# Attention scores at even steps only, and query scores in four passes a block that DVE adds up

## The chip, the cores and the metric

The kernel runs on one core of one Trainium2 chip. The metric is the device time of one execution in microseconds, median over the runs.

## The reference

Agent attention, then a feed-forward network with gelu on its output. Four batches, 12480 tokens, 128 channels, 49 agents; 2048 hidden units.

```python
def _attn_ref(q, k, v, agents):
    scale = 1.0 / np.sqrt(q.shape[-1])
    def sm(a, b):
        s = scale * (a @ b.transpose(0, 2, 1))
        s = s - s.max(-1, keepdims=True)
        e = np.exp(s)
        return e / (e.sum(-1, keepdims=True) + 1e-09)
    a2k = sm(agents, k)
    agent_v = a2k @ v
    q2a = sm(q, agents)
    return (q2a @ agent_v).astype(np.float32)

def _moe_ref(x, w_in, w_out):
    h = x @ w_in
    g = h * (1.0 / (1.0 + np.exp(-1.702 * h)))
    return (g @ w_out).astype(np.float32)
```

## The kernel before

All engines work in an order that is written out by hand. The unit of work on queries is a group of 960 tokens (13 a batch, 52 in all). For each group the feed-forward network runs over 16 blocks of 128 hidden units, the **steps**; `two_steps(t)` issues two of them, a **double step**, and eight double steps make a **cycle**. The agents' values are multiplied into `w_in` once a batch (`weights_part`), so the up projection takes the softmaxed query scores directly.

In a double step TensorE (PE) does in this order: four matmuls of 480 columns (L407) and four row-tiled ones on 19 rows (L410, the **quad**), the jobs put at the even step, six **downs** (L445: `gh` with `wo_h`, `gl` with `wo_h`, `gh` with `wo_l`, each for two halves of the group) of one of the steps four back, the jobs put at the odd step (`second`), and the six downs of the other step. ACT applies gelu (L420) to the four results and rounds every second one to `gh` (L430); a DMA issued by POOL rounds the others. DVE makes the remainder `gl = g - gh` (L435) of each step, one of the two behind the jobs of the even step and one behind those of the odd step.

The attention work of later groups and of the next batch is put at steps by the table `at`. At step f of a cycle (f = t mod 16):

- query scores for the group after next at `Q_AT` = 12 (first half of its 8 blocks of 120 tokens) and 13 (second half), split into three bf16 parts by four DVE pieces at 8 to 11 (L173, L175); the maximum and its subtraction (`query_shift`, L350 and L352) at 14, exp at the next 0, sums and normalization at 2, transposes (L379) at `P_AT` = 4.
- key scores of the next batch, 13 blocks, each in two halves at the next two free steps, even or odd (`pe_step`); then `key_store`: ACT copies the bank to `score` (L228) and DVE takes the running maximum from the same bank (L225).
- after the last key block its maximum, then values (`key_values`, L284, 8 passes of 258 columns) at steps 6 and 11 of the next six to seven cycles, with `value_pair` (L279, L280) four steps ahead of them into a single buffer `v_pair`; then the weights (L330).

So a batch passes through a key phase (about five cycles, the first in the start), a value phase (about six) and a weights phase (two); the last 13 cycles have no next batch and none of it. Here they are called late cycles.

A score is the sum of six products of bf16 parts, accumulated by six matmuls of 49 columns in one bank; each loads its own weights (the token block):

```python
products = [(x0, 0), (x0, 1), (x0, 2), (x1, 0), (x1, 1), (x2, 0)]
```

The score, key maximum, transposes, values and weights share two PSUM banks (`ps_m`).

Of the kernel before, what the change touches and what calls it, by code (L numbers as in the profile page):

```python
# [8 lines left out]
F32 = mybir.dt.float32  # L9
# [5 lines left out]
ALU = mybir.AluOpType  # L15
AX = mybir.AxisListType

P = 128
TB = 120
KB = 8  # L20
# [7 lines left out]
Q_AT = 12  # L28
E_AT = 0
P_AT = 4  # L30
S_AT = 8
K_AT = 3
V_AT = (6, 11)
V_LAST = 5
R = 30
FIRST_WORDS = 1
FIRST_UP = 2
# [6 lines left out]
def kernel(  # L44
# [10 lines left out]
    nc = tc.nc  # L55
    B, C, N = qT.shape
    A = agT.shape[2]
    F = w_in.shape[1] // 2
    NF = F // P
    NG = N // GT  # L60
    NKG = N // (TB * KB)
# [11 lines left out]
    ps_m = ctx.enter_context(tc.tile_pool(name="ps_m", bufs=2, space=bass.MemoryType.PSUM))  # L73
# [10 lines left out]
    for c in range(2):  # L84
        nc.vector.tensor_add(
            out=sel[:, c * H : c * H + A], in0=ident[:, 0:A], in1=ident[:, H : H + A]
# [3 lines left out]
    for i in range(2):  # L90
        t = const.tile([P, KB, P], F32R, name=f"e_pair{i}")
# [8 lines left out]
    e_sb = const.tile([P, KB, A + 1], F32, name="e_sb")  # L100
# [5 lines left out]
    score = const.tile([P, NKG * KB, A], F32, name="score")  # L106
# [44 lines left out]
    ag_part = const.tile([P, B, 3, A], BF16, name="ag_part")  # L151
# [27 lines left out]
    def scores(b, parts, ps, c):  # L179
        x0, x1, x2 = parts  # L180
        for j in range(c * KB // 2, (c + 1) * KB // 2):
            t = slice(j * TB, j * TB + P)
            o = ps[:, j * A : (j + 1) * A]
            products = [(x0, 0), (x0, 1), (x0, 2), (x1, 0), (x1, 1), (x2, 0)]
            for i, (x, y) in enumerate(products):
                nc.tensor.matmul(  # L186
                    out=o,
                    lhsT=x[:, t],
                    rhs=ag_part[:, b, y, :],
                    start=(i == 0),  # L190
                    stop=(i == len(products) - 1),
                )

    def score_bank():
        ps = ps_m.tile([P, 512], F32, name="ps_m")
        return ps, ps[:TB, : KB * A].rearrange("p (j a) -> p j a", a=A)
# [24 lines left out]
    def running_max(g, s):  # L221
        if g == 0:
            nc.vector.tensor_copy(out=run_max[:TB], in_=s)
        else:
            nc.vector.tensor_tensor(out=run_max[:TB], in0=s, in1=run_max[:TB], op=ALU.max)  # L225

    def key_store(g, s):
        nc.scalar.copy(out=score[:TB, g * KB : (g + 1) * KB, :], in_=s)  # L228
        running_max(g, s)

    def key_max_0(d):
        mx = work.tile([P, A], F32, name="mx", bufs=1)
        nc.vector.tensor_reduce(out=mx[:TB], in_=run_max[:TB].rearrange("p j a -> p a j"), axis=AX.X, op=ALU.max)
        d["mx"] = mx
# [36 lines left out]
    def key_pair(g):  # L271
        sc = score[:TB, g * KB : (g + 1) * KB, :]
        ep = e_pair[g % 2]
        nc.vector.tensor_copy(out=ep[:TB, :, 0:A], in_=sc)
        nc.vector.tensor_sub(out=ep[:TB, :, H : H + A], in0=sc, in1=ep[:TB, :, 0:A].bitcast(F32))
# [67 lines left out]
    def query_load(b, g):  # L343
        t = loads.tile([P, GT + PAD], F32, name="qt", tag="qt", bufs=1)
        nc.sync.dma_start(out=t[:, 0:GT], in_=qT[b, :, g * GT : (g + 1) * GT])
        return t

    def query_shift(s):
        m = work.tile([P, KB], F32, name="m")
        nc.vector.tensor_reduce(out=m[:TB], in_=s, axis=AX.X, op=ALU.max)  # L350
        sd = e_sb[:TB, :, 0:A]
        nc.vector.tensor_tensor(  # L352
            out=sd, in0=s, in1=m[:TB].unsqueeze(2).broadcast_to([TB, KB, A]), op=ALU.subtract
        )
        return sd

# [109 lines left out]
    q_parts = {}  # L466
    scored = {}
    banks = {}
# [5 lines left out]
    def do_key_load(b, g):  # L474
        if b < B and g < NKG:
            kts[b, g] = key_load(b, g)
# [5 lines left out]
    def do_query_load(n):  # L482
        if n < B * NG:
            qts[n] = query_load(*divmod(n, NG))

    def do_key_split(b, g, i):
        if i == 0:
            k_parts[b, g], pieces[b, g] = split(kts.pop((b, g)))
        pieces[b, g](i)
# [7 lines left out]
    def do_key_scores(b, g, c):  # L497
        if c == 0:
            banks[b, g] = score_bank()
        scores(b, k_parts[b, g], banks[b, g][0], c)  # L500

    def do_key_store(b, g):
        key_store(g, banks.pop((b, g))[1])

    def do_key_values(b, g):
        sums[b, g] = key_values(g)
# [5 lines left out]

    def do_query_scores(n, c):
        if n < B * NG:
            if c == 0:
                banks[n] = score_bank()
            scores(n // NG, q_parts[n], banks[n][0], c)

    def do_query_shift(n):
        if n < B * NG:  # L520
            scored[n] = query_shift(banks.pop(n)[1])

    def do_query_exp(n):
        if n < B * NG:
# [57 lines left out]
    for g in range(NKG):  # L582
# [3 lines left out]
        for j in range(KB):  # L586
            nc.tensor.matmul(
                out=acc_ps[:A, : C + 1],
                lhsT=score[:TB, g * KB + j, :],
                rhs=vt[:TB, j, :],  # L590
                start=(g == 0 and j == 0),
                stop=(g == NKG - 1 and j == KB - 1),
# [23 lines left out]
    steps = B * NG * NF  # L616
    per_batch = NG * NF
    at = {}
    pe_steps = {n * NF + f for n in range(B * NG) for f in (Q_AT, Q_AT + 1, P_AT)}

    def put(t, fn):
        at.setdefault(t, []).append(fn)


    def pe_step(t):
        while t in pe_steps:
            t += 1
        pe_steps.add(t)
        return t
# [7 lines left out]
    for b in range(B - 1):  # L637
        s0 = b * per_batch
        done = s0
        for k in range(NKG):  # L640
            t = pe_step(s0 + (11 + 5 * k if b == 0 else K_AT + 11 * k // 2))
            t1 = pe_step(t + 1)
            put(t - 13 if b else max(t - 13, 0), lambda b=b, k=k: do_key_load(b + 1, k))
            begin = max(t - 4, done + 1)
            for i in range(4):
                put(min(begin + i, t - 1 if i < 2 else t1 - 1), lambda b=b, k=k, i=i: do_key_split(b + 1, k, i))
            done = t1
            put(t, lambda b=b, k=k: do_key_scores(b + 1, k, 0))
            put(t1, lambda b=b, k=k: do_key_scores(b + 1, k, 1))
            put(t1 + 1, lambda b=b, k=k: do_key_store(b + 1, k))  # L650
        mx = {}
        put(t1 + 2, lambda mx=mx: key_max_0(mx))
        t = pe_step(t1 + 3)
        put(t, lambda mx=mx: key_max_1(mx))
        t = pe_step(t + 2)
        put(t, lambda mx=mx: key_max_2(mx))
        shift = t + 1

        g0 = (shift + 1 - s0 - E_AT + NF - 1) // NF
        for k in range(NKG):  # L660
            slot = s0 + (g0 + k // 2) * NF + E_AT
            exps.setdefault(slot, []).append(k)
            last = k == NKG - 1
            t = slot + (V_LAST if last else V_AT[k % 2])
            put(min(shift + 3 * k, slot - 1), lambda k=k: key_shift(k, nc.vector.tensor_tensor))
            put(t - 16, lambda b=b, k=k: do_value_load(b + 1, k))
            put(t - 4, lambda b=b, k=k: value_pair(vts.pop((b + 1, k))))
            put(slot + 3 - last, lambda k=k: key_pair(k))
            assert t not in pe_steps
            put(t, lambda b=b, k=k: do_key_values(b + 1, k))  # L670
            put(t + 1, lambda b=b, k=k: do_key_sum(b + 1, k))
        w = {}
        put(t + 2, lambda b=b, w=w: weights_0(accs.pop(b + 1), w))
        t = pe_step(t + 3)
        put(t, lambda w=w: weights_1(w))
        for c in range(F // 512):
            t = pe_step(t + (3 if c else 1))
            assert t < s0 + per_batch + 4 * c - 5, (b, shift - s0, g0, t - s0)
            put(t, lambda b=b, w=w, c=c: weights_part(b + 1, w, c))
    for n in range(B * NG):  # L680
        s0 = n * NF
        if n:
            put(s0 + E_AT, lambda n=n: do_query_exp(n + 1))
            if s0 + E_AT in exps:
                ks = exps[s0 + E_AT]
                put(s0 + E_AT, lambda ks=ks: key_exp(ks[0], len(ks)))
            put(s0 + E_AT + 2, lambda n=n: do_query_sums(n + 1))
            put(s0 + E_AT + 2, lambda n=n: do_query_softmax(n + 1))
        put(s0 + P_AT, lambda n=n: do_query_pairs(n + 1))
        for i in range(4):  # L690
            put(s0 + S_AT + i, lambda n=n, i=i: do_query_split(n + 2, i))
        for c in range(2):
            put(s0 + Q_AT + c, lambda n=n, c=c: do_query_scores(n + 2, c))
        put(s0 + Q_AT + 2, lambda n=n: do_query_load(n + 3))
        put(s0 + Q_AT + 2, lambda n=n: do_query_shift(n + 2))


    E = mybir.EngineType
    g = {}
# [98 lines left out]
```

## Time and profile before

| | |
|---|---|
| median of 3 runs | 2039.23 us (2039.01 to 2040.26) |
| the profiled execution | 2040.92 us |
| its span, first to last instruction | 2039.1 us |
| PE busy, share of the span | 1992.4 us, 98% |
| DVE busy | 1576.9 us, 77% |
| ACT busy | 1440.2 us, 71% |
| POOL busy | 281.4 us, 14% |

Busy time of PE counts a matmul from its start to its modelled end, so it is no measure of how well the array is used; the chain of work that ended last and the starts of instructions in the time line say more. Bf16 passes overlap one another: the pace is read from one start to the next.

### The profile page before, as it was taken

The page shows a single profiled execution, that of the slowest core. Times are in us where ns is not written, and L with a number is a line of the kernel's source. Part 1 is how long each engine was busy: PE and PEld are TensorE (multiplying, and loading weights), DVE is VectorE, ACT ScalarE, POOL GpSimd, SP SyncE. Part 2 cuts the span into 40 slices and gives each one's busy share as a digit, 9 for nine tenths or more (in the row PEclk, how much of TensorE's full clock was granted, in tenths as well). Part 3 has the DMA queues.
Part 4 walks back from the last instruction along what each step waited for, and adds up shares of the span by engine and source line. Part 5 has one row for each costly group of instructions (what it writes and reads, how often), then busy time and mean ns, then how long its engine had stood idle before and what let it go on. Part 6 is the DMA issues. An engine that isn't in the chain of part 4 may idle for free.

```text
span 2039.1 us, 36417 instructions
## 1 busy us (share of the span) xinstructions
PE 1992.4 (98%) x13688; PEld 1525.2 (75%) x13688; DVE 1576.9 (77%) x2025; ACT 1440.2 (71%) x2457; POOL 281.4 (14%) x594
## 2 busy tenths in 40 slices
PE   8789999999999999999999999999999999999999
PEld 7567777777777777777777777777777777777776
DVE  4788888888777879888777888888877776767665
ACT  3256677677776777777776677777777877777775
POOL 3011111111111111111111111111111111111111
PEclk9799999999999999999999999999999999999999
DMA  9645556565455565565555555566545545455443
GB/s 252 180 157 182 180 181 184 172 190 174 159 170 174 181 191 181 173 190 175 170 172 171 180 190 175 170 191 174 170 164 161 178 156 170 155 171 165 161 157 134
DMA packets 129444, 356.00 MB, mean 175 GB/s; under 512 B 15696, under 2 KB 48688, under 8 KB 129268
## 3 DMA queue, kind: packets, MB, share of 16 engines
q0 software_dynamic: 67520, 230.22, 34.4%
q1 hardware_dynamic: 61748, 123.46, 20.9%
q8 instruction: 108, 1.77, 0.4%
q14 instruction: 68, 0.56, 0.1%
HBM read 80.97 MB, written 25.56 MB: 52 GB/s over the span
## 4 chain that ended last, share of the span: by engine, by line
PE 89%; DVE 5%; ACT 2%; DMA 2%; issue 1%; POOL 1%; SPq 0%; ACTq 0%; POOLq 0%; DVEq 0%
PE po L445 53%; PE ph L407 17%; PE ph L410 8%; PE ps_m L186 6%; PE ps_m L284 2%; DVE gl L435 1%; DMA gh<-g 1%; PE ps_m L379 1%; PE ps_m L209 1%; ACT g L420 1%; PE ps_m L330 1%; DVE rest L173 1%; DVE rest L175 1%; POOL score L265 1%; DMA words<-w_in 0%
## 5 line engine op out<-in xcount | busy, mean ns | idle before, releaser
L420 ACT ACTIVATE g<-ph 128x480 f32<-128x480 f32 x1664 | 816.6, 577 | 494.4 <-PE ph L410 489.3
L435 DVE TENSOR_TENSOR gl<-g,gh 128x960 fp32r<-128x960 f32 x832 | 941.3, 1153 | 192.5 <-DMA gh<-g 101.9
L445 PE MATMUL po<-gh,wo_h 128*128 128x480 f32 x1664 | 551.7, 413 | 1.9 <-DMA gh<-g 1.9
L445 PE MATMUL po<-gl,wo_h 128*128 128x480 f32 x1664 | 502.1, 383 | 4.9 <-DVE gl L435 4.3
L445 PE MATMUL po<-gh,wo_l 128*128 128x480 f32 x1664 | 500.2, 382 | 0.0
L426 POOL DMA_DIRECT2D gh<-g x468 | 252.0, 538 | 1689.9 <-ACT g L420 1129.2
L445 PEld LDWEIGHTS po<-gl,wo_h 128*128 128x128 f32 x1664 | 311.6, 189 | 63.0 <-DVE gl L435 14.9
L445 PEld LDWEIGHTS po<-gh,wo_l 128*128 128x128 f32 x1664 | 314.0, 189 | 49.8
L445 PEld LDWEIGHTS po<-gh,wo_h 128*128 128x128 f32 x1664 | 273.2, 189 | 85.4 <-issue 64.8
L407 PE MATMUL ph<-sa,wh 128*128 128x480 f32 x832 | 319.8, 384 | 4.8 <-ACT g L420 3.3
L407 PE MATMUL ph<-sb,wh 128*128 128x480 f32 x832 | 321.6, 386 | 0.0
L430 ACT CAST gh<-g 128x960 fp32r<-128x960 f32 x312 | 311.8, 999 | 9.0
L410 PE MATMUL ph<-rq,wq 19*128 19x480 f32 x1664 | 205.2, 481 | 0.0
L407 PEld LDWEIGHTS ph<-sa,wh 128*128 128x128 f32 x832 | 157.4, 189 | 37.4 <-ACT g L420 11.0
L407 PEld LDWEIGHTS ph<-sb,wh 128*128 128x128 f32 x832 | 157.2, 189 | 35.4 <-ACT g L420 11.6
L410 PEld LDWEIGHTS ph<-rq,wq 19*128 19x128 f32 x1664 | 80.0, 182 | 137.0 <-issue 136.5
L186 PE MATMUL ps_m<-ag_part,rest 128*128 128x49 bf16 x2184 | 130.3, 185 | 6.6 <-DVE rest L175 6.4
L175 DVE TENSOR_TENSOR rest<-rest 128x480 bf16<-128x480 f32 (+1 forms) x182 | 129.8, 719 | 0.4
L186 PEld LDWEIGHTS <-rest 128*128 128x128 bf16 x2184 | 109.4, 97 | 8.4 <-DVE rest L175 7.8
L225 DVE TENSOR_TENSOR run_max<-ps_m,run_max 120x392 f32<-120x392 f32 x36 | 20.4, 567 | 79.3 <-ACT score L228 79.1
L186 PEld LDWEIGHTS <-qt 128*128 128x128 bf16 x1248 | 61.3, 98 | 25.1 <-issue 25.0
L186 PE MATMUL ps_m<-ag_part,qt 128*128 128x49 bf16 x1248 | 74.6, 186 | 0.0
(97 smaller groups left out, 1326.8 us busy)
## 6 DMA issues: line engine op xcount, KB each, us to landing
gh<-g POOLq DMA_DIRECT2D x468, 480.0 KB, 3.6
kt<-kT SPq DMA_DIRECT2D x52, 480.0 KB
qt<-qT SPq DMA_DIRECT2D x52, 480.0 KB
vt<-v SPq DMA_DIRECT2D x52, 480.0 KB
outT<-o SPq DMA_DIRECT2D x104, 240.0 KB
rq<-sa SPq DMA_DIRECT2D x104, 35.6 KB
rq<-sb SPq DMA_DIRECT2D x104, 35.6 KB
sa<-sa SPq DMA_DIRECT2D x104, 28.1 KB
```

Source lines behind the costliest of these rows:

```text
L173: nc.vector.tensor_sub(out=r[:, s], in0=t[:, s], in1=halves(t)[0][:, s])
L175: nc.vector.tensor_sub(out=halves(r)[1][:, s], in0=r[:, s], in1=halves(r)[0][:, s])
L186: nc.tensor.matmul(out=o, lhsT=x[:, t], rhs=ag_part[:, b, y, :], start=(i == 0), stop=(i == len(products) - 1),)
L225: nc.vector.tensor_tensor(out=run_max[:TB], in0=s, in1=run_max[:TB], op=ALU.max)
L284: nc.tensor.matmul(out=ps[:, : 2 * C + 2], lhsT=e_pair[g % 2][:TB, j, :], rhs=v_pair[:TB, j, :], start=(first and j == 0), stop=(last and ...
L407: nc.tensor.matmul(out=ph[k][:, :CH], lhsT=wh[:, cols[i]], rhs=pairs[c], start=True, stop=False)
L410: nc.tensor.matmul(out=ph[k][:, :CH], lhsT=wq[r, cols[i]], rhs=rq[r], start=False, stop=True, tile_position=(k * 32, 0),)
L420: nc.scalar.activation(out=gs[i][:, c, :], in_=ph[k][:, :CH], func=AF.Gelu_apprx_sigmoid)
L426: nc.gpsimd.dma_start(out=gh, in_=g)
L430: nc.scalar.copy(out=gh, in_=g)
L435: nc.vector.tensor_sub(out=gl, in0=g, in1=gh.bitcast(F32))
L445: nc.tensor.matmul(out=po[c][:, :CH], lhsT=lhsT[:, f, :], rhs=rhs[:, c, :], start=(begin and first), stop=(end and last),)
```

## The change

Query scores: a block of 120 tokens gets four passes instead of six, into two columns for each agent (98 columns a block). The high part of the tokens meets agent parts 0 and 1 in one pass of 98 columns, part 2 in one of 49 into the second column; the middle part meets 0 and 1 in one of 98; the low part meets 0 in one of 49. Eight blocks now fill two banks (`score_halves`), and DVE adds the two columns (two `tensor_reduce`) before the maximum. All query scores stand at step 12, the shift at 13, and the next query load at 13.

Key scores: both halves of a block at one even step, from the tables `K_FIRST` and `K_AT`; ACT's copy at the step after, the running maximum one step later still and from `score`. `pe_step` gives even steps alone. Values go to 6 and 10.

```diff
-K_AT = 3
-V_AT = (6, 11)
-V_LAST = 5
+K_FIRST = (10, 16, 22, 26, 32, 38, 42, 48, 54, 58, 62, 66, 70)
+K_AT = (6, 10, 16, 22, 26, 32, 38, 42, 48, 54, 58, 64, 70)
+V_AT = (6, 10)
...
+    def score_halves(b, parts, c):
+        x0, x1, x2 = parts
+        a = ag_part[:, b].rearrange("p i a -> p (i a)")
+        mm = nc.tensor.matmul
+        ps = ps_m.tile([P, 512], F32, name="ps_m")
+        for j in range(KB // 2):
+            t0 = (c * KB // 2 + j) * TB
+            t = slice(t0, t0 + P)
+            o = ps[:, j * 2 * A : (j + 1) * 2 * A]
+            mm(out=o, lhsT=x0[:, t], rhs=a[:, 0 : 2 * A], start=True, stop=False)
+            mm(out=o[:, A:], lhsT=x0[:, t], rhs=a[:, 2 * A :], start=False, stop=False)
+            mm(out=o, lhsT=x1[:, t], rhs=a[:, 0 : 2 * A], start=False, stop=False)
+            mm(out=o[:, 0:A], lhsT=x2[:, t], rhs=a[:, 0:A], start=False, stop=True)
+        return ps[:TB, : KB * A].rearrange("p (j i a) -> p j a i", i=2, a=A)
...
     def key_store(g, s):
         nc.scalar.copy(out=score[:TB, g * KB : (g + 1) * KB, :], in_=s)
-        running_max(g, s)
...
-    def query_shift(s):
+    def query_shift(halves):
+        sd = e_sb[:TB, :, 0:A]
+        for c, s in enumerate(halves):
+            o = sd[:, c * KB // 2 : (c + 1) * KB // 2, :]
+            nc.vector.tensor_reduce(out=o, in_=s, axis=AX.X, op=ALU.add)
         m = work.tile([P, KB], F32, name="m")
-        nc.vector.tensor_reduce(out=m[:TB], in_=s, axis=AX.X, op=ALU.max)
-        sd = e_sb[:TB, :, 0:A]
+        nc.vector.tensor_reduce(out=m[:TB], in_=sd, axis=AX.X, op=ALU.max)
         nc.vector.tensor_tensor(
-            out=sd, in0=s, in1=m[:TB].unsqueeze(2).broadcast_to([TB, KB, A]), op=ALU.subtract
+            out=sd, in0=sd, in1=m[:TB].unsqueeze(2).broadcast_to([TB, KB, A]), op=ALU.subtract
         )
         return sd
...
-    pe_steps = {n * NF + f for n in range(B * NG) for f in (Q_AT, Q_AT + 1, P_AT)}
+    pe_steps = {n * NF + f for n in range(B * NG) for f in (Q_AT, P_AT)}
...
     def pe_step(t):
-        while t in pe_steps:
+        while t % 2 or t in pe_steps:
             t += 1
         pe_steps.add(t)
         return t
...
         for k in range(NKG):
-            t = pe_step(s0 + (11 + 5 * k if b == 0 else K_AT + 11 * k // 2))
-            t1 = pe_step(t + 1)
+            t = s0 + (K_AT if b else K_FIRST)[k]
+            assert pe_step(t) == t
             put(t - 13 if b else max(t - 13, 0), lambda b=b, k=k: do_key_load(b + 1, k))
             begin = max(t - 4, done + 1)
             for i in range(4):
-                put(min(begin + i, t - 1 if i < 2 else t1 - 1), lambda b=b, k=k, i=i: do_key_split(b + 1, k, i))
-            done = t1
-            put(t, lambda b=b, k=k: do_key_scores(b + 1, k, 0))
-            put(t1, lambda b=b, k=k: do_key_scores(b + 1, k, 1))
-            put(t1 + 1, lambda b=b, k=k: do_key_store(b + 1, k))
+                put(min(begin + i, t - 1), lambda b=b, k=k, i=i: do_key_split(b + 1, k, i))
+            done = t
+            for c in range(2):
+                put(t, lambda b=b, k=k, c=c: do_key_scores(b + 1, k, c))
+            put(t + 1, lambda b=b, k=k: do_key_store(b + 1, k))
+            put(t + 2, lambda k=k: running_max(k, score[:TB, k * KB : (k + 1) * KB, :]))
...
         for c in range(2):
-            put(s0 + Q_AT + c, lambda n=n, c=c: do_query_scores(n + 2, c))
-        put(s0 + Q_AT + 2, lambda n=n: do_query_load(n + 3))
-        put(s0 + Q_AT + 2, lambda n=n: do_query_shift(n + 2))
+            put(s0 + Q_AT, lambda n=n, c=c: do_query_scores(n + 2, c))
+        put(s0 + Q_AT + 1, lambda n=n: do_query_load(n + 3))
+        put(s0 + Q_AT + 1, lambda n=n: do_query_shift(n + 2))
```

The order on the engines shows what that moves. On PE, in a key phase before the change, at the border of the two halves of a key block (`rest` and `kt` are parts of the key block, `po0` and `po1` the two output halves):

```order
L186 LDWEIGHTS rest_7213
L186 MATMUL ps_m_7259<-ag_part_106,rest_7213 128x49
L445 MATMUL po0_7153<-gh_7151,wo_h_101 128x480
L445 MATMUL po1_7154<-gh_7151,wo_h_101 128x480
L445 MATMUL po0_7153<-gl_7222,wo_h_101 128x480
L445 MATMUL po1_7154<-gl_7222,wo_h_101 128x480
L445 MATMUL po0_7153<-gh_7151,wo_l_102 128x480
L445 MATMUL po1_7154<-gh_7151,wo_l_102 128x480
L186 LDWEIGHTS kt_6848
L186 MATMUL ps_m_7259<-ag_part_106,kt_6848 128x49
```

After the change, at the end of a key block (L463 is the former L445):

```order
L186 LDWEIGHTS rest_7197
L186 MATMUL ps_m_7322<-ag_part_106,rest_7197 128x49
L463 MATMUL po0_6932<-gh_7236,wo_h_101 128x480
L463 MATMUL po1_6933<-gh_7236,wo_h_101 128x480
L463 MATMUL po0_6932<-gl_7287,wo_h_101 128x480
L463 MATMUL po1_6933<-gl_7287,wo_h_101 128x480
```

The six downs that stood between the halves now follow the whole block.

On DVE, around the query shift of a late cycle, before (the last split piece, the remainders, the shift, the sums of the exponentials):

```order
L175 TENSOR_TENSOR rest<-rest 128x480
L435 TENSOR_TENSOR gl<-g,gh 128x960 x3
L350 TENSOR_REDUCE m<-ps_m 120x8
L352 TENSOR_TENSOR e_sb<-ps_m,m 120x8x49
L435 TENSOR_TENSOR gl<-g,gh 128x960 x4
L362 TENSOR_REDUCE z<-e_sb 120x8
L363 RECIPROCAL z<-z 120x8
```

and after (L453 is the former L435; L367, L369 and L370 are the shift, L380 the sums):

```order
L175 TENSOR_TENSOR rest<-rest 128x480
L453 TENSOR_TENSOR gl<-g,gh 128x960 x2
L367 TENSOR_REDUCE e_sb<-ps_m 120x4x49 x2
L369 TENSOR_REDUCE m<-e_sb 120x8
L370 TENSOR_TENSOR e_sb<-e_sb,m 120x8x49
L453 TENSOR_TENSOR gl<-g,gh 128x960 x5
L380 TENSOR_REDUCE z<-e_sb 120x8
L381 RECIPROCAL z<-z 120x8
```

The shift stands one remainder further ahead and has two reductions more; five remainders instead of four follow until the sums.

On DVE in a key phase before, from the last split piece through the shift (L225 is the running maximum, from the bank):

```order
L175 TENSOR_TENSOR rest<-rest 128x480
L350 TENSOR_REDUCE m<-ps_m 120x8
L352 TENSOR_TENSOR e_sb<-ps_m,m 120x8x49
L435 TENSOR_TENSOR gl<-g,gh 128x960 x2
L225 TENSOR_TENSOR run_max<-ps_m,run_max 120x392
L435 TENSOR_TENSOR gl<-g,gh 128x960
```

and after (L241 is the former L225, now from `score`; the second split piece of the next key block stands right ahead of the reductions):

```order
L453 TENSOR_TENSOR gl<-g,gh 128x960
L241 TENSOR_TENSOR run_max<-score,run_max 120x392
L173 TENSOR_TENSOR rest<-kt 128x488
L453 TENSOR_TENSOR gl<-g,gh 128x960
L175 TENSOR_TENSOR rest<-rest 128x488
L367 TENSOR_REDUCE e_sb<-ps_m 120x4x49 x2
L369 TENSOR_REDUCE m<-e_sb 120x8
L370 TENSOR_TENSOR e_sb<-e_sb,m 120x8x49
L453 TENSOR_TENSOR gl<-g,gh 128x960
```

The running maximum, which stood in the step of ACT's copy, is ahead of the next block's split one step after it, and the reductions wait for the whole run of query scores.

## Rows read from the trace of the kernel before

**Rows 1.** The page, parts 1 and 4: busy time, the last chain.

```profile
PE 1992.4 (98%) x13688; PEld 1525.2 (75%) x13688; DVE 1576.9 (77%) x2025; ACT 1440.2 (71%) x2457; POOL 281.4 (14%) x594
...
PE 89%; DVE 5%; ACT 2%; DMA 2%; issue 1%; POOL 1%; SPq 0%; ACTq 0%; POOLq 0%; DVEq 0%
```

**Rows 2.** Time line of PE, cycle 42: start, duration, engine, operation, count.

```profile
1711.52 0.38 PE L407 MATMUL ph<-sa,wh 128*128 128x480 f32 x1
...
1712.91 0.25 PE L186 MATMUL ps_m<-ag_part,qt 128*128 128x49 bf16 x3
...
1713.54 0.68 PE L445 MATMUL po<-gh,wo_h 128*128 128x480 f32 x2
1714.05 0.60 PE L445 MATMUL po<-gl,wo_h 128*128 128x480 f32 x2
...
1716.94 0.39 PE L407 MATMUL ph<-sa,wh 128*128 128x480 f32 x1
...
1718.32 0.70 PE L445 MATMUL po<-gh,wo_h 128*128 128x480 f32 x2
1718.87 0.60 PE L445 MATMUL po<-gl,wo_h 128*128 128x480 f32 x2
...
1720.19 0.60 PE L445 MATMUL po<-gl,wo_h 128*128 128x480 f32 x2
...
1721.06 0.38 PE L407 MATMUL ph<-sa,wh 128*128 128x480 f32 x1
```

**Rows 3.** Time line of PE, cycle 19: double steps 6 and 10 (values).

```profile
841.72 0.39 PE L407 MATMUL ph<-sa,wh 128*128 128x480 f32 x1
...
846.81 0.38 PE L407 MATMUL ph<-sa,wh 128*128 128x480 f32 x1
...
850.93 0.38 PE L407 MATMUL ph<-sa,wh 128*128 128x480 f32 x1
...
856.00 0.39 PE L407 MATMUL ph<-sa,wh 128*128 128x480 f32 x1
```

**Rows 4.** Windows: key phases, first value cycle, five late cycles.

```profile
175.00:294.90 119.90, 117.20 (x1048) 89.08 (x1047) 97.61 (x132) 83.54 (x144) 15.50 (x38) 1.00 0.56 178
596.70:791.30 194.60, 193.22 (x1687) 146.82 (x1686) 160.54 (x212) 138.50 (x239) 25.77 (x63) 1.00 0.56 180
791.30:828.40 37.10, 37.10 (x229) 28.41 (x228) 32.59 (x43) 27.41 (x47) 5.02 (x10) 1.00 0.61 180
1089.30:1284.70 195.40, 193.18 (x1687) 146.64 (x1686) 160.14 (x212) 138.45 (x239) 25.76 (x63) 1.00 0.56 180
1625.50:1798.40 172.90, 172.90 (x1061) 132.40 (x1060) 122.06 (x140) 133.21 (x226) 24.36 (x51) 1.00 0.50 165
```

The columns of rows 4: from and to, length, busy us of PE, PEld, DVE, ACT and POOL with counts, PEclk, DMA share, GB/s.

**Rows 5.** Who waited for whom: us in total, times, longest.

```profile
DVE run_max L225 <- ACT score L228: 79.1, 35, 4.8
...
PEld po L445 <- DVE gl L435: 14.9, 34, 3.4
```

**Rows 6.** Time line in a key phase; idle time before in brackets.

```profile
625.71 0.57 DVE L225 TENSOR_TENSOR run_max<-ps_m,run_max 120x392 f32<-120x392 f32 x1 [2.54 <-ACT score L228]
...
628.54 0.30 PEld L445 LDWEIGHTS po<-gl,wo_h 128*128 128x128 f32 x2 [0.29 <-DVE gl L435]
```

**Rows 7.** Groups of DVE by form: count, busy us, mean ns.

```profile
L435 DVE TENSOR_TENSOR gl<-g,gh 128x960 fp32r<-128x960 f32 x832 | 941.3, 1153 | 192.5 <-DMA gh<-g 101.9 <-ACT gh L430 41.3 <-PE ph L407 35.3
...
L350 DVE TENSOR_REDUCE m<-ps_m 120x8 f32<-120x392 f32 x52 | 29.2, 561 | 13.5 <-PE ps_m L186 13.3
...
L233 DVE TENSOR_REDUCE mx<-run_max 120x49 f32<-120x392 f32 x4 | 3.4, 840 | 0.0
```

**Rows 8.** The page, part 5: ACT's gelu, weight loads of scores.

```profile
L420 ACT ACTIVATE g<-ph 128x480 f32<-128x480 f32 x1664 | 816.6, 577 | 494.4 <-PE ph L410 489.3
...
L186 PEld LDWEIGHTS <-rest 128*128 128x128 bf16 x2184 | 109.4, 97 | 8.4 <-DVE rest L175 7.8
```

**Rows 9.** The chain that ended last, at the start.

```profile
77.24 0.47 DVE m L350
```

More of the change, by code (lines that the diff above doesn't have):

```diff
@@ L514, in do_query_scores @@
         if n < B * NG:
-            if c == 0:
-                banks[n] = score_bank()
-            scores(n // NG, q_parts[n], banks[n][0], c)
+            banks.setdefault(n, []).append(score_halves(n // NG, q_parts[n], c))
     def do_query_shift(n):
         if n < B * NG:
-            scored[n] = query_shift(banks.pop(n)[1])
+            scored[n] = query_shift(banks.pop(n))
     def do_query_exp(n):
@@ L645 @@
             for i in range(4):
-                put(min(begin + i, t - 1 if i < 2 else t1 - 1), lambda b=b, k=k, i=i: do_key_split(b + 1, k, i))
-            done = t1
-            put(t, lambda b=b, k=k: do_key_scores(b + 1, k, 0))
-            put(t1, lambda b=b, k=k: do_key_scores(b + 1, k, 1))
-            put(t1 + 1, lambda b=b, k=k: do_key_store(b + 1, k))
+                put(min(begin + i, t - 1), lambda b=b, k=k, i=i: do_key_split(b + 1, k, i))
[4 more added lines that the diff above has]
+            put(t + 2, lambda k=k: running_max(k, score[:TB, k * KB : (k + 1) * KB, :]))
         mx = {}
-        put(t1 + 2, lambda mx=mx: key_max_0(mx))
-        t = pe_step(t1 + 3)
+        put(t + 2, lambda mx=mx: key_max_0(mx))
+        t = pe_step(t + 3)
         put(t, lambda mx=mx: key_max_1(mx))
@@ L662 @@
             exps.setdefault(slot, []).append(k)
-            last = k == NKG - 1
-            t = slot + (V_LAST if last else V_AT[k % 2])
+            t = slot + V_AT[k % 2]
             put(min(shift + 3 * k, slot - 1), lambda k=k: key_shift(k, nc.vector.tensor_tensor))
@@ L667 @@
             put(t - 4, lambda b=b, k=k: value_pair(vts.pop((b + 1, k))))
-            put(slot + 3 - last, lambda k=k: key_pair(k))
+            put(slot + 3, lambda k=k: key_pair(k))
             assert t not in pe_steps
```

## The prediction

> **What bounds the kernel now.** I read the page first. TensorE (PE) is busy 98% of the span and holds 89% of the chain that ended last; DVE is next with 77% [rows 1]. So the end moves with what PE has to do and with the few places where it waits. I then read PE's own time line in a cycle with no keys in it [rows 2]. A cycle is 16 steps (one group of 960 queries), a double step begins with the first L407. The plain double step, 1716.94 to 1721.06, is 4.12 us; the one with the query scores, 1711.52 to 1716.94, is 5.42. PE has no gap in either: scores lie on the path and cost 1.30 us a cycle. Third, the windows of whole phases [rows 4]: five late cycles take 172.9 us, 34.58 each, all at a granted clock of 1.00 (2.4 GHz). Five cycles that also score the next batch's keys take 194.6, more than their passes explain (below). There I read the waits and the time line [rows 5, 6]: PE waits for DVE's gl, while DVE itself stands still for ACT's copy of the key scores, 79.1 us in 35 waits.
>
> **The change, part by part.** Sums are against the profiled execution's span of 2039.1 us (its own time is 2040.92; the median of the runs shown is 2039.23, nearly the span, so I take the difference off the median).
>
> *Query scores, 50 in the loop.* Before, two runs of 24 passes. The first stands behind the quad: 1712.91 to 1713.54, 0.63 us, 26.2 ns a pass; the first pair of downs after it takes 0.51 us where a pair straight behind a quad takes 0.55 [rows 2], so this place costs 0.59. The second run, between the two groups of downs, has the rest of the 1.30: 0.71. After, one run behind the quad of 8 blocks with two passes of 49 columns and two of 98. The 49-column ones keep 26.2 ns. For 98 columns no row exists. Below: 98 columns at the granted 2.4 GHz, 40.8 ns. Above: twice 26.2, 52.4 ns, when nothing is gained but the place. Nearest row: the value passes, 258 columns with a weight load each; a double step with eight of them is 5.07 to 5.09 against 4.12 [rows 2, 3], 0.12 us a pass, of which 98/258 is 45 ns. I take 45: 8 x (52.4 + 90) ns = 1.14, less 0.04, 1.10 us instead of 1.30. **50 x 0.20 = -10.0 us**, with ends -13.5 (40.8 ns) and -4.0 (52.4).
>
> The Trainium skill speaks against the wide passes: its page "TensorE: Matmul & The Clock Gate", section "Back-to-back issue gap", gives streams of a weight load and a matmul about 81 ns at 128 columns and 131 at 512, a straight line that would be about 77 ns at 98, and by it the query scores would cost 16 us more in all instead of 10 less. The same line gives about 71 ns at 49 columns, where the trace has 26.2.
>
> *Key scores, 39 blocks.* Still six passes, but both halves in one run at an even step. In the order before, 34 of the 78 halves stand behind a quad and 44 between the downs: 34 x 0.59 + 44 x 0.71 = 51.3 us. After: 39 x (1.26 - 0.04) = 47.6. **-3.7 us.**
>
> *Values.* 21 runs go from step 11 to step 10. The two places give 5.07 and 5.09 us [rows 3]: **+0.4 us**. The load of v_pair (L279, L280) goes from step 7 to 6; it has to wait for the passes of step 6 to read the single buffer, and one gl more is queued behind it; that gl is taken in the next double step, so I price it at nothing, and in the range below with DVE.
>
> *Key maximum.* The running maximum (L225; I keep its price for its new source) moves from the step of ACT's copy to the step after, and reads the copy. The time line shows what it did: DVE idle 2.54 us for ACT at 625.71, then PE idle 0.29 at 628.54 for a gl [rows 6]. ACT's copy stands behind four gelus of 0.58 us [rows 8], which begin 1.4 us into the double step when the quad is done, and a cast; so it ends in the last part of a double step that is 5.3 long, and the maximum, queued in the next one, mostly finds it done. What is it worth? The excess of the three key windows over late cycles is 194.6 - 172.9 = 21.7, 22.5 and (three cycles) 119.9 - 103.7 = 16.2 us [rows 4]. The passes in them, 11, 11 and 8 halves at 0.59 and 15, 15 and 9 at 0.71, are 17.1, 17.1 and 11.1. About 15 us stay, 1 of it the transposes of the maximum, which no group prices: 14 us of waits. DVE is also given more work and the scores come in bigger lumps, so I take half: **-7 us**, ends 0 and -14.
>
> *Two more reductions on DVE, 52 times.* Each reads 392 PSUM values in pairs 49 apart and writes 196. The nearest row is L350, 561 ns for as many inputs; with a stride, L233 takes 840 [rows 7]. I take 0.56 each, since its source is PSUM as L350's is: +1.1 us a cycle (1.7 at the other end). In late cycles DVE is busy 122 of 172.9 us, and the work is hidden by idle time: nothing. In key windows 160.5 of 195, it would be 166 to 169 of some 190. In the first value cycle of a batch 32.6 of 37.1 us, it becomes 33.7 to 34.3 of 36.9 [rows 4]; for six such cycles I add **+1 us** (0 to +6.7, all of it exposed). At the start the chain runs over DVE, through the queries' own maximum at 77.24 us [rows 9]; two extra reductions there are **+1.1 us** (0 to +2.2, if those of the first block show as well).
>
> *Banks and loads.* The query scores now take both ps_m banks in one double step; the second bank was last used by the run at step 10, whose reader (ACT's copy or DVE's sum at step 11) has most of a double step. The query load moves one step earlier on SP and keeps some 9 steps until its split. Nothing for both.
>
> Sum: -10.0 - 3.7 + 0.4 - 7 + 1 + 1.1 = **-18.2 us**: 2039.2 - 18.2 = **2021 us**.
>
> **The rivals.** *DVE keeps the waits* (18 in 100). The key waits stay as long as they are, since the queue is fuller (160.5 of 195 us busy already), and the first value cycles lose 3: -10 - 3.7 + 0.4 + 1.1 + 3 = -9.2, 2030 us. For it: waits of PE end in DVE's gl [rows 5, 6]. Against: DVE's own largest stand-still is the one that is taken out.
>
> *Nothing gained by width* (7 in 100). A 98-column pass takes twice a 49-column one, and the waits stay: -4 - 3.7 + 0.4 + 1.1 + 3 = -3, 2036 us. Against it is the column time of the 258-column passes [rows 3].
>
> *Slower, through DVE's queue at step 13* (6 in 100). The four operations of the shift wait until the whole run of scores is done, some 1.4 + 1.1 = 2.5 us into the double step, and then hold DVE for 4 x 0.56 = 2.2; the gl of step 10 (1.15 [rows 7]) stands behind them and ends at 5.9, 0.7 into the next double step, which takes it 3.25 us after its start (1720.19 against 1716.94 [rows 2]). So 2.5 us are to spare. In the 32 cycles of key and value phases a lag of DVE beyond that costs PE one for one: 1 us each is +32, 2053 us; from 0.57 us a cycle on the change loses. Against: DVE's share in those cycles is at most 93%.
>
> *Slower, through the weight loads* (3 in 100). A wide pass that could not hide its load would take the load's recorded 97 ns [rows 8]: 8 x (52.4 + 194) ns = 1.97, +0.64 a cycle, +32 in place of -10, 2063 us. The rule of the Trainium skill named above ("TensorE: Matmul & The Clock Gate", "Back-to-back issue gap") would be a milder form of this, with about 2047. Against: the same 97 ns loads vanish behind 26.2 ns passes now.
>
> **How the numbers follow.** The forecast has 66 in 100, from 2013 to 2029 us. The range reaches from its lower end into the first rival and short of the second: 2012 to 2034. A measurement of this kernel tells 0.2%, 4 us, from no change. Faster than 2035.1: the forecast and the first rival, 0.84. Same: 0.07, the rival on width. Slower: 0.09.
>
> **What would show it.** Late cycles: the double step with query scores at about 5.22 us instead of 5.42, the others at 4.12; this alone tests the width. Key scores: 5.34 us in a double step without waits. The waits of the maximum for ACT at well under half of 79 us. L350's kind three times a cycle, 0.56 us each. In key windows some 190 us instead of 195. I am wrong if late cycles gain less than 0.1 us, if key windows do not shrink, or if PE shows new waits for gl in the double step after step 12.

## The result, and the profile after

The changed kernel takes 2015.41 us, median of 4 runs (2014.86 to 2015.93), against 2039.12 for the kernel before: ratio 0.9883, 95% interval 0.9868 to 0.9899. It is 23.7 us faster where 18.2 were forecast. The profiled execution took 2015.93 us, its span 2014.1.

The page, parts 1 and 4, which answer to [rows 1]:

```profile
span 2014.1 us, 34876 instructions
...
PE 1972.2 (98%) x12856; PEld 1527.8 (76%) x12856; DVE 1636.8 (81%) x2129; ACT 1439.8 (71%) x2457; POOL 285.9 (14%) x594
...
PE 85%; DVE 4%; DMA 4%; issue 3%; ACT 2%; POOL 1%; SPq 0%; ACTq 0%; POOLq 0%; DVEq 0%
```

DVE got 60 us more to do, and PE still holds the chain. PE's time line in cycle 42 (L425 begins a double step, L204 is the first pass of the query scores, L463 are the downs), which answers to [rows 2]:

```profile
1687.94 0.39 PE L425 MATMUL ph<-sa,wh 128*128 128x480 f32 x1
...
1689.33 0.22 PE L204 MATMUL ps_m<-ag_part,qt 128*128 128x98 bf16 x1
...
1690.47 0.68 PE L463 MATMUL po<-gh,wo_h 128*128 128x480 f32 x2
...
1693.19 0.38 PE L425 MATMUL ph<-sa,wh 128*128 128x480 f32 x1
...
1697.29 0.39 PE L425 MATMUL ph<-sa,wh 128*128 128x480 f32 x1
```

The 32 passes take 1690.47 - 1689.33 = 1.14 us, 142.5 ns a block; less two passes of 26.2 ns, a wide one takes 45 ns. The double step is 5.25 us, the plain one behind it 4.10.

The windows that answer to [rows 4], with the same columns: three key windows, the first value cycle, five late cycles:

```profile
171.90:287.00 115.10, 114.59 (x1024) 90.83 (x1023) 102.12 (x139) 83.97 (x145) 15.40 (x38) 1.00 0.64 188
586.00:775.90 189.90, 189.06 (x1608) 148.77 (x1607) 165.96 (x222) 138.92 (x239) 25.55 (x63) 1.00 0.63 188
775.90:813.00 37.10, 37.10 (x213) 28.32 (x212) 33.80 (x45) 27.21 (x47) 5.50 (x10) 1.00 0.59 178
1073.30:1262.50 189.20, 188.31 (x1607) 148.28 (x1606) 165.78 (x222) 138.89 (x239) 25.55 (x63) 1.00 0.63 189
1602.30:1774.40 172.10, 172.10 (x982) 132.50 (x981) 127.69 (x150) 133.28 (x226) 24.41 (x51) 1.00 0.52 166
```

The key windows together went from 509.9 to 494.2 us, a late cycle from 34.58 to 34.42, the first value cycle stayed at 37.1. The waits that answer to [rows 5]:

```profile
DVE run_max L241 <- ACT score L244: 29.4, 11, 3.0
...
PEld po L463 <- DVE gl L453: 13.3, 19, 3.3
```

DVE's stand-still at the running maximum fell from 79.1 us to 29.4. The new reduction among DVE's groups, which answers to L350 in [rows 7]:

```profile
L367 DVE TENSOR_REDUCE e_sb<-ps_m 120x196 f32<-120x392 f32 x104 | 54.3, 559 | 2.2 <-PE ps_m L207 1.5
```

It costs 559 ns, as L350 did, in spite of the stride. Three stretches outside these windows changed too: the start with cycle 0, cycle 1, and the weights cycles of the first batch. Before and after:

```profile
0.00:132.30 132.30, 103.07 (x768) 85.90 (x769) 85.89 (x150) 47.11 (x94) 25.03 (x49) 0.83 0.73 199
132.30:175.00 42.70, 40.01 (x382) 30.54 (x380) 34.69 (x47) 28.04 (x49) 5.15 (x13) 1.00 0.55 179
517.30:596.70 79.40, 76.42 (x448) 56.79 (x447) 54.48 (x68) 55.82 (x96) 9.80 (x20) 0.98 0.50 160
```

```profile
0.00:133.90 133.90, 102.47 (x721) 85.45 (x722) 93.37 (x162) 46.89 (x94) 25.14 (x49) 0.83 0.73 198
133.90:171.90 38.00, 38.00 (x342) 30.18 (x341) 32.83 (x46) 27.91 (x49) 5.14 (x13) 1.00 0.61 189
509.80:586.00 76.20, 74.99 (x415) 55.75 (x414) 56.39 (x72) 55.44 (x96) 10.29 (x20) 1.00 0.50 158
```

The account of the 25.0 us of span: key windows -15.7, cycle 1 -4.7, first weights cycles -3.2, late cycles about -1.7, value cycles (18) -1.9, start +1.6; the rest is rounding and the other weights cycles.

### The profile page after: what moved, and what is told of

Read it like the earlier page. It is cut to its first block, busy times and chain, and to the rows that moved or that the text cites. A ratio compares the mean times of both kernels' runs of the same rounds, so it can differ in the third digit from the quotient of the medians.

```text
span 2014.1 us, 34876 instructions
## 1 busy us (share of the span) xinstructions
PE 1972.2 (98%) x12856; PEld 1527.8 (76%) x12856; DVE 1636.8 (81%) x2129; ACT 1439.8 (71%) x2457; POOL 285.9 (14%) x594
## 4 chain that ended last, share of the span: by engine, by line
PE 85%; DVE 4%; DMA 4%; issue 3%; ACT 2%; POOL 1%; SPq 0%; ACTq 0%; POOLq 0%; DVEq 0%
PE po L463 51%; PE ph L425 16%; PE ph L428 8%; DMA gh<-g 3%; PE ps_m L186 2%; PE ps_m L299 2%; DVE gl L453 2%; ACT g L438 1%; PE ps_m L204 1%; PE ps_m L225 1%; PE ps_m L397 1%; PE ps_m L206 1%; POOL score L280 1%; PE ps_m L205 1%; PE ps_m L207 0%
## 5 line engine op out<-in xcount | busy, mean ns | idle before, releaser
L453 DVE TENSOR_TENSOR gl<-g,gh 128x960 fp32r<-128x960 f32 x832 | 941.5, 1152 | 161.9 <-DMA gh<-g 118.6
L463 PE MATMUL po<-gh,wo_h 128*128 128x480 f32 x1664 | 540.2, 406 | 0.0
L463 PE MATMUL po<-gl,wo_h 128*128 128x480 f32 x1664 | 500.5, 382 | 5.8 <-DVE gl L453 5.6
L463 PE MATMUL po<-gh,wo_l 128*128 128x480 f32 x1664 | 500.4, 382 | 0.0
L444 POOL DMA_DIRECT2D gh<-g x468 | 256.5, 548 | 1656.0 <-ACT g L438 1108.1
L463 PEld LDWEIGHTS po<-gl,wo_h 128*128 128x128 f32 x1664 | 312.5, 189 | 62.4 <-DVE gl L453 13.3
L463 PEld LDWEIGHTS po<-gh,wo_l 128*128 128x128 f32 x1664 | 314.1, 189 | 49.8
L463 PEld LDWEIGHTS po<-gh,wo_h 128*128 128x128 f32 x1664 | 283.6, 189 | 82.4 <-issue 55.8
L425 PE MATMUL ph<-sa,wh 128*128 128x480 f32 x832 | 319.6, 384 | 4.4 <-ACT g L438 3.2
L425 PE MATMUL ph<-sb,wh 128*128 128x480 f32 x832 | 321.4, 386 | 0.0
L425 PEld LDWEIGHTS ph<-sa,wh 128*128 128x128 f32 x832 | 157.6, 189 | 36.9 <-ACT g L438 10.9
L425 PEld LDWEIGHTS ph<-sb,wh 128*128 128x128 f32 x832 | 157.2, 189 | 34.6 <-ACT g L438 10.9
L175 DVE TENSOR_TENSOR rest<-rest 128x488 bf16<-128x488 f32 (+1 forms) x182 | 129.8, 721 | 0.9
L173 DVE TENSOR_TENSOR rest<-qt 128x488 f32<-128x488 f32 x104 | 67.9, 654 | 0.0
L409 DVE TENSOR_TENSOR sa<-ps_m,sa 49x480 fp32r<-49x480 f32 x52 | 33.8, 651 | 37.0 <-ACT sb L407 36.4
L204 PE MATMUL ps_m<-ag_part,qt 128*128 128x98 bf16 x416 | 63.0, 207 | 0.7 <-DVE wl L348 0.7
```

The costliest lines, as they stand in the source:

```text
L173: nc.vector.tensor_sub(out=r[:, s], in0=t[:, s], in1=halves(t)[0][:, s])
L175: nc.vector.tensor_sub(out=halves(r)[1][:, s], in0=r[:, s], in1=halves(r)[0][:, s])
L204: mm(out=o, lhsT=x0[:, t], rhs=a[:, 0 : 2 * A], start=True, stop=False)
L425: nc.tensor.matmul(out=ph[k][:, :CH], lhsT=wh[:, cols[i]], rhs=pairs[c], start=True, stop=False)
L444: nc.gpsimd.dma_start(out=gh, in_=g)
L453: nc.vector.tensor_sub(out=gl, in0=g, in1=gh.bitcast(F32))
```

## The experiments

In the table, the waits in the key windows are an estimate: their sum less what late cycles and passes explain. Before, 509.9 us hold about 14 of waits by the prediction's count, so 496 would be free of them. From that, whole blocks at even steps take 3.7, the query scores in one run 0.10 x 13 = 1.3, the wide passes 0.07 x 13 = 0.9 (both measured below). Each kernel was compared with the kernel before on its own chip.

| kernel | us | ratio to before, 95% interval | key windows, us | waits in them |
|---|---|---|---|---|
| before | 2039.1 | | 509.9 | 14 |
| changed | 2015.4 | 0.9883 (0.9868 to 0.9899) | 494.2 | 4 |
| six passes | 2018.0 | 0.9889 (0.9874 to 0.9904) | 495.5 | 4.5 |
| maximum with the copy | 2017.7 | 0.9887 (0.9872 to 0.9901) | 497.3 | 7 |
| both: places alone | 2021.9 | 0.9909 (0.9894 to 0.9924) | 499.1 | 8 |
| before, maximum later | 2025.0 | 0.9922 (0.9905 to 0.9939) | 498.3 | 2 |
| copy and maximum at an even step | 2080.7 | 1.0197 (1.0171 to 1.0223) | 551.7 | 62 |
| copy even, maximum odd | 2023.1 | 0.9915 (0.9898 to 0.9931) | 502.7 | 13 |
| sums twice | 2015.7 | 0.9879 (0.9864 to 0.9893) | 494.6 | 4.5 |
| values at 10 and 18 | 2001.2 | 0.9806 (0.9792 to 0.9821) | | |
| the same, first keys later | 2001.3 | 0.9805 (0.9789 to 0.9822) | | |

The sums of the three key windows of four runs, in the table's order: six passes, maximum with the copy, places alone, copy even with maximum odd.

```profile
sum 495.50, PE 493.33 PEld 389.25 DVE 421.21 ACT 362.18 POOL 66.65; mean PE 164.44 PEld 129.75 DVE 140.40 ACT 120.73 POOL 22.22
```

```profile
sum 497.30, PE 493.35 PEld 388.20 DVE 432.09 ACT 361.73 POOL 66.65; mean PE 164.45 PEld 129.40 DVE 144.03 ACT 120.58 POOL 22.22
```

```profile
sum 499.10, PE 495.06 PEld 389.77 DVE 418.60 ACT 361.80 POOL 66.36; mean PE 165.02 PEld 129.92 DVE 139.53 ACT 120.60 POOL 22.12
```

```profile
sum 502.70, PE 495.20 PEld 387.42 DVE 432.96 ACT 360.35 POOL 66.34; mean PE 165.07 PEld 129.14 DVE 144.32 ACT 120.12 POOL 22.11
```

**Six passes in one run.** Query scores as before, but all at step 12:

```diff
-            banks.setdefault(n, []).append(score_halves(n // NG, q_parts[n], c))
+            if c == 0:
+                banks[n] = score_bank()
+            scores(n // NG, q_parts[n], banks[n][0], c)
...
-    def query_shift(halves):
+    def query_shift(s):
...
```

The part that is left out of the diff is the shift of before, with the maximum taken straight from the one bank.

> The changed kernel, but with the query scores of before: six passes of 49 columns a block into one bank, no sums on DVE; still in one run at step 12. If the wide passes earn what the late cycles of the changed kernel show, the double step with query scores goes from 5.25 to about 5.33 us in late cycles, and the whole is about 4 us over the changed kernel (50 x 0.08), 2019 us. Rival: the two sums cost on DVE, in key and value cycles, what the passes save on PE; then the whole is at 2015 us or less, with late cycles longer and the others shorter.

It took 2017.97 us. PE's time line in a late cycle of it (L422 begins a double step):

```profile
1688.75 0.38 PE L422 MATMUL ph<-sa,wh 128*128 128x480 f32 x1
...
1690.13 0.25 PE L186 MATMUL ps_m<-ag_part,qt 128*128 128x49 bf16 x3
...
1691.38 0.68 PE L460 MATMUL po<-gh,wo_h 128*128 128x480 f32 x2
...
1694.07 0.39 PE L422 MATMUL ph<-sa,wh 128*128 128x480 f32 x1
```

The run of 48 passes takes 1.25 us and the double step 5.32: against 5.42 the one place gives 0.10, against 5.25 the width gives 0.07. The whole is 2.6 us over the changed kernel, less than the two intervals can tell apart; 50 x 0.07 = 3.5 by the time line. So in late cycles the width pays, by the time line, and the whole gives no sign that the sums on DVE take it back.

**The maximum with the copy.**

```diff
         nc.scalar.copy(out=score[:TB, g * KB : (g + 1) * KB, :], in_=s)
+        running_max(g, s)
...
-            put(t + 2, lambda k=k: running_max(k, score[:TB, k * KB : (k + 1) * KB, :]))
```

> The changed kernel, but with the running maximum back in the step of ACT's copy and reading the bank. Theory: most of what the key phases gained came from taking DVE's wait for that copy away; then the five key cycles go from 190 us back to 194 or more in each batch, the waits of the maximum to 60 us or more, and the whole is 12 to 16 us over the changed kernel, about 2029. Rival: the gain of the key phases came from the places of the key blocks (whole blocks, evenly spread, at even steps); then the whole is within 4 us of the changed kernel, 2015 to 2019, even where DVE waits.

2017.67 us, 2.3 over the changed kernel: the rival's time, and not the theory's. DVE's wait is nearly back, as its row shows:

```profile
DVE run_max L241 <- ACT score L244: 52.3, 35, 3.5
```

52.3 us of stand-still, and yet only some 3 us more of waits on the path. So the length of DVE's stand-still is not what it costs.

**Before, with the maximum later.**

```diff
             put(t1 + 1, lambda b=b, k=k: do_key_store(b + 1, k))
+            put(t1 + 2, lambda k=k: running_max(k, score[:TB, k * KB : (k + 1) * KB, :]))
...
-        running_max(g, s)
```

> The kernel before with one edit: the running maximum one step after ACT's copy, from the copy. Theory of the wait: it gains 8 to 14 us by itself, 2025 to 2031, all in key phases. Rival of the places: it gains 3 us or less, 2036 to 2039, since the key halves still stand where DVE's and ACT's work is dense.

2024.98 us, 15.6 under the kernel before on the same chip (2040.6). Here the theory of the wait holds, and by a little more than its range. Its key windows and its wait:

```profile
172.30:287.60 115.30, 115.30 (x1047) 89.17 (x1046) 96.66 (x130) 83.11 (x144) 15.49 (x38) 1.00 0.60 185
589.30:780.50 191.20, 191.20 (x1688) 147.40 (x1687) 161.51 (x212) 138.00 (x239) 25.77 (x63) 1.00 0.57 183
1078.20:1270.00 191.80, 190.93 (x1687) 147.28 (x1686) 161.19 (x212) 137.91 (x239) 25.76 (x63) 1.00 0.56 183
```

```profile
DVE run_max L225 <- ACT score L228: 51.1, 28, 3.7
```

Again DVE stands still for 51 us, and PE is busy through the whole of two of the three windows. Both runs together: either part of the change takes away most of the harm, so their gains don't add. On top of the new places the later maximum is worth some 4 us (2021.9 with the places alone, the next run, against 2018.0 with six passes).

**The places alone**, the edits of the first two runs together.

> The changed kernel with query scores in six passes and the running maximum in the step of the copy, both as before: the places alone are left of the change. If the places do most of it, 2018 to 2022 (the six-pass run and the run with the maximum back were 2.5 and 2 us over the changed kernel). If the two parts taken back cover for each other, 2025 or more.

2021.90 us, as expected if the places do most: the new places, query scores in one run included, are worth some 18.7 us against the kernel before on its chip (2040.65), with 8 us of waits left.

**Copy and maximum at an even step.** Why is the stand-still harmless in the changed places? There the copy is put at an odd step, where DVE has the even step's jobs and one remainder ahead of the maximum. This run puts it back at the head of an even step, in the new places; the edit is on top of the run with the maximum with the copy:

```diff
-            put(t + 1, lambda b=b, k=k: do_key_store(b + 1, k))
+            put(t + (1 if t % NF == 10 else 2), lambda b=b, k=k: do_key_store(b + 1, k))
```

> As the run with the maximum in the step of the copy, but copy and maximum are put two steps after the scores, an even step, for key blocks at steps 0 and 6 (those at 10 stay, because of the bank). There the maximum is the first thing that DVE does in a double step while ACT's copy is behind four gelus, as in the kernel before; at an odd step one of the two remainders is ahead of it. If the harm of the wait lies in what is queued behind it, the five key cycles take 193 us or more instead of 190.5 and the whole is 5 to 10 us above that run, 2023 to 2028. If whole blocks at even steps make the wait harmless anyway, it stays within 2 us of that run, 2016 to 2020.

2080.67 us, 63 us over the run with the maximum at the odd step. The direction is the theory's; the size is many times what I expected. The time line at 671 us shows one case (idle time before in brackets):

```profile
671.76 0.52 ACT L244 COPY score<-ps_m 120x392 f32<-120x392 f32 x1
...
672.31 0.57 DVE L241 TENSOR_TENSOR run_max<-ps_m,run_max 120x392 f32<-120x392 f32 x1 [3.35 <-ACT score L244]
672.79 0.72 DVE L175 TENSOR_TENSOR rest<-rest 128x488 bf16<-128x488 f32 x1
...
675.75 0.11 PEld L186 LDWEIGHTS <-rest 128*128 128x128 bf16 x2 [1.01 <-DVE rest L173]
```

DVE stands 3.35 us for ACT's copy, which is behind four gelus; behind the maximum stand the next key block's split pieces, and PE, now at that block, waits 1.01 us for one of them and 0.62 for the next. The four largest rows of what PE's matmuls waited for in the whole execution (`p_pad` holds the normalized query scores that are transposed at step 4):

```profile
PE po L464 <- DVE gl L454: 13.2, 21, 2.8
...
PE ps_m L186 <- DVE rest L175: 11.7, 24, 0.5
PE ps_m L398 <- DVE p_pad L387: 11.7, 14, 0.9
...
PE ps_m L186 <- DVE rest L173: 11.2, 13, 1.0
```

That is 47.8 us; the same four rows sum to 8.7 us in the run with the maximum at the odd step. All four end in operations of DVE's queue, and no wait of PE ends in the maximum or in ACT's copy, so PE did not wait for the bank that both read. Another part is TensorE's clock, the number behind the five busy times in the three key windows:

```profile
178.10:309.00 130.90, 121.86 (x1024) 94.52 (x1024) 100.58 (x138) 84.42 (x145) 15.35 (x38) 0.96 0.55 166
606.60:816.80 210.20, 195.18 (x1607) 149.78 (x1606) 164.93 (x222) 139.45 (x239) 25.51 (x63) 0.99 0.55 170
1115.20:1325.80 210.60, 195.69 (x1608) 150.64 (x1607) 164.85 (x222) 139.54 (x239) 25.50 (x63) 0.98 0.55 170
```

In the changed kernel it is 1.00 in all of them. Seven double steps of this run, at steps 4 and 10, have a granted clock of 0.78 to 0.80 and last 7.8 and 8.6 us, where most others at these steps last 6.5 and 7.1: some 10 us in all, by estimate. The four executions lie in the order of their mean clock, from 2074.2 us at 0.985 to 2088.0 at 0.977.

**Copy even, maximum odd.** Is it DVE's place in the queue, or that the copy itself is later?

```diff
+            late = 1 if t % NF == 10 else 2
-            put(t + 1, lambda b=b, k=k: do_key_store(b + 1, k))
-            put(t + 2, lambda k=k: running_max(k, score[:TB, k * KB : (k + 1) * KB, :]))
+            put(t + late, lambda b=b, k=k: do_key_store(b + 1, k))
+            put(t + late + 1, lambda k=k: running_max(k, score[:TB, k * KB : (k + 1) * KB, :]))
...
-        put(t + 2, lambda mx=mx: key_max_0(mx))
+        put(t + 3, lambda mx=mx: key_max_0(mx))
```

> The changed kernel with ACT's copy two steps after the scores for key blocks at steps 0 and 6, as in the run with copy and maximum at an even step, but the maximum (from the copy) another step later, at the odd step, where a remainder of DVE is ahead of it. That run took 65 us more than the changed kernel. If what it lost came from DVE standing at the maximum with its queue behind it, this one is back within 5 us of the changed kernel, 2013 to 2020. If it came from the later copy (the bank comes free later, ACT's own casts are pushed back), it stays above 2050.

2023.06 us: 58 of the 65 us are back. It ends 3 us above the expected range, so the later copy, with a later maximum, costs some 8 by itself. The rest of the harm is in what is queued behind the maximum. One thing more differs between the two runs: the maximum reads the copy here and the bank there. No run changed the source alone; that the bank is not at fault rests on the rows of PE's waits above.

**Sums twice.**

```diff
             nc.vector.tensor_reduce(out=o, in_=s, axis=AX.X, op=ALU.add)
+            nc.vector.tensor_reduce(out=o, in_=s, axis=AX.X, op=ALU.add)
```

> The changed kernel with each of the two sums of query scores done twice on DVE, 1.1 us more a cycle; the output is the same. If DVE has room, as the sum of the prediction has it, the whole stays within 3 us of the changed kernel, 2014 to 2019, and late cycles at 34.4 us. If DVE is near its limit in key and value cycles, each of 34 such cycles loses up to 1.1 us, and the whole is at 2025 or more.

2015.66 us, the changed kernel's time. Its longest key window:

```profile
585.80:776.00 190.20, 189.19 (x1608) 148.81 (x1607) 171.11 (x233) 138.83 (x239) 25.51 (x63) 1.00 0.63 188
```

With 171.1 us busy of 190.2 DVE still hides them.

**Values at steps 10 and 18.** In value cycles of the changed kernel the double step at 4 is 5.03 us or more, where late cycles have 4.48; ACT's two exps and two table loads from step 0 are not done in time.

```diff
-V_AT = (6, 10)
+V_AT = (10, 18)
```

> The changed kernel with the values at steps 10 and 2 of the next cycle (18) in place of 6 and 10. In value cycles PE waits about 0.6 us, sometimes 1.2, at step 4 for ACT, which has two exps and two table loads to do from step 0. Theory: a value run of 0.97 us at step 2 gives ACT the time, so the double step at 4 falls from 5.06 or 5.72 to 4.49 in some 18 cycles, and the whole falls by 8 to 13 us, to 2002 to 2007. Rival: PE's wait there ends in DVE's remainder, whose input comes by DMA, and only moves to another step; then 2012 to 2016.

2001.15 us, 14.3 under the changed kernel, a little more than the theory's range, and the fastest here. The double step at 4 of cycle 20, first changed, then with the values moved:

```profile
858.07 0.38 PE L425 MATMUL ph<-sa,wh 128*128 128x480 f32 x1
858.29 0.47 PE L425 MATMUL ph<-sb,wh 128*128 128x480 f32 x1
...
863.14 0.38 PE L425 MATMUL ph<-sa,wh 128*128 128x480 f32 x1
```

```profile
850.52 0.38 PE L425 MATMUL ph<-sa,wh 128*128 128x480 f32 x1
850.75 0.38 PE L425 MATMUL ph<-sb,wh 128*128 128x480 f32 x1
...
855.03 0.38 PE L425 MATMUL ph<-sa,wh 128*128 128x480 f32 x1
```

5.07 us became 4.51: the second to fourth up matmuls, which came every 0.45 us behind ACT's gelus, come every 0.22. The value run itself costs what it did. ACT's gelus of the double step before, behind the exps, in the same order:

```profile
857.19 1.96 ACT L438 ACTIVATE g<-ph 128x480 f32<-128x480 f32 x4
```

```profile
848.64 1.96 ACT L438 ACTIVATE g<-ph 128x480 f32<-128x480 f32 x4
```

Changed, they end at 859.15, 1.08 us after PE began step 4; with the values moved, at 850.60, 0.08 us after. ACT's work is the same in both; it got 0.97 us of PE's time in which to do it. The rival, a wait that only moves to another step, is out.

**The same, first keys later.**

```diff
-K_FIRST = (10, 16, 22, 26, 32, 38, 42, 48, 54, 58, 62, 66, 70)
+K_FIRST = (16, 18, 22, 26, 32, 38, 42, 48, 54, 58, 62, 66, 70)
```

> The run with values at 10 and 18, with the first two key blocks of the first batch at steps 16 and 18 in place of 10 and 16. In cycle 0 DVE is busy throughout with converting weights, and the splits of the first block stand in it. If DVE is the limit there, cycles 0 and 1 together fall by 1.5 to 3 us and the whole to 1998 to 2000. If not, 2001 as that run.

2001.30 us, no gain: by the starts of the double steps, cycle 0 fell from 55.6 to 53.7 us and cycle 1 rose from 38.0 to 39.9. Some 1.2 us of that are the passes of the first key block itself, which moved with it from cycle 0 to cycle 1. Whether DVE limits cycle 0 is not shown.

## Why the prediction was right, step by step

The whole lies inside the range, and the prices of the passes came out nearly as worked out. That it is within 6 us of the forecast is in part luck: the query scores gave 1.5 us less, the waits some 7 more, cycle 1 counted in, and 3.2 came from a stretch that no term covers.

*Query scores* (-10.0): the pass was right to the nanosecond, 45 by the time line, and the double step 5.25 instead of the forecast 5.22, since the downs behind the run gain 0.02 less than before. That is 50 x 0.17 = -8.5. The prediction put 0.12 of the 0.20 on the width and 0.08 on the place; measured apart, 0.07 is the width and 0.10 the place. The rule of the Trainium skill ("TensorE: Matmul & The Clock Gate", "Back-to-back issue gap"), read along a straight line between its two figures, would have the wide pass near 77 ns, an estimate. The pass took 45, and the measurement decides.

*Key scores* (-3.7) and *values* (+0.4): double steps with 48 passes are 5.30 to 5.38 us where nothing waits, as forecast, and the two value runs take the same time at both steps; neither sum was measured by itself. Of the 21 value runs 18 go from step 11 to step 10; the last run of each of the three batches stood at step 5 before, not at 6 or 11, and goes to 6.

*Key maximum* (-7): the term that was mis-sized. It took half of the 14 us of waits, and no row spoke for the half. The key windows lost about 10 of the 14, and cycle 1, which is a key cycle as well and which the count left out with the start, fell by another 4.7 (by 2.8 where the maximum alone was moved). Its reason was half right. The wait for ACT's copy did the harm, as the runs with the maximum later and with it at the head of an even step show; but the move of the maximum was not the only thing that cured it. The new places, with the copy at an odd step, nearly do it alone; which of them (whole blocks, even steps, the steps of the split pieces) does it was not run apart. The argument pointed at DVE's idle time (79.1 us) and asked whether it falls; its length is not what counted, but what stood behind it in the queue.

*Reductions on DVE* (+1 and +1.1): 559 ns each, at the lower price; in key and value cycles the runs show no cost, and none of doubling them. (The first term counts six first value cycles; there are three.) Five value cycles of the changed kernel have a longer double step at 4, 5.31 to 5.82 us, but the run with the maximum with the copy, which has the same sums, has none. The sign that was named, new waits in the double step after step 12, did not show: it takes 4.07 to 4.12 us in key cycles that put nothing else there. Start and cycle 0 together are 1.6 us longer, but that does not show the +1.1: the first double step begins at 75.8 to 78.8 us in the runs with the new places, and at 78.0 with the sums twice.

*Not foreseen*: 3.2 us in the first batch's weights cycles. Before, one double step there lasted 7.9 us, while PE waited for a gh by DMA:

```profile
583.57 0.71 PE L445 MATMUL po<-gh,wo_h 128*128 128x480 f32 x2 [1.94 <-DMA gh<-g]
...
584.83 1.17 PE L445 MATMUL po<-gl,wo_h 128*128 128x480 f32 x2 [0.56 <-DVE gl L435]
```

Behind these two waits the granted clock fell: it is 0.86 in this double step and 0.90 in the next, and seven passes of 480 columns took from 584.83 to 587.79, where they take 0.22 each at 1.00. That is some 1.4 of the 3.2 us, by estimate. Weights were moved by DMA in the same stretch, and in the changed order their parts stand at other steps. Runs with the new places have 76 us there (75 with the values at 10 and 18), the run with the old places 79; which of the moves collides was not tried.

## What to carry to other kernels

In an engine with a fixed order, price a wait by what is queued behind it and by when the next engine needs that, not by how long the engine stands: 52 us of idle time cost some 3; with the same operation one step later, at the head of a double step, DVE stood for 110 us, and the whole grew by another 63. Two edits that cure the same wait don't add, so each must be run alone before either is believed. When the busiest engine waits for another one's burst, moving its own independent work into that gap, 0.97 us of value passes here, was worth more than the cheaper passes.

## What the runs showed of the hardware

A bf16 pass with its own weight load took 26.2 ns at 49 columns and 45 ns at 98 at a granted clock of 1.00, although the load is recorded with 97 ns. A DVE reduction of 392 values from PSUM took 559 to 561 ns whether it makes 8 results of 49 neighbours or 196 of two values 49 apart; L233, from SBUF with eight values 49 apart, took 840. TensorE's granted clock fell behind some of its waits, to the lower of its two levels (1.2 in place of 2.4 GHz): in the kernel before after 1.94 and 0.56 us of standing, with passes of 480 columns 0.40 to 0.49 us apart instead of 0.22; with copy and maximum at an even step in seven double steps, while most double steps there with waits of the same kind kept 1.00.
